# A fifth buffer for the split numerators, a sixth instead of a seventh for x, and another order of the convolution's last stages

## The chip, the cores and the metric

The kernel runs on one core of a Trainium2 chip. The metric is device time in microseconds of one launch; the kernel before was run three times, and one further execution was profiled.

## The reference

Two stages follow each other. The first is a causal convolution over the sequence with 7 taps, whose weights are a softmax per head (8 heads of 24 columns, d_model 192, 8 sequences of 4160 rows). The second treats the 33280 rows as tokens of one SoLU layer with 1024 hidden columns.

```python
w = softmax(weight)                                  # 8 heads x 7 taps
out[b, s, h, :] = sum_k w[h, k] * x_pad[b, s + k, h, :]
x = out.reshape(B * S, D)                            # 33280 x 192
h = x @ w_in                                         # 192 x 1024
sm = exp(h - max(h)); sm = sm / (sum(sm) + 1e-9)
solu = h * sm
ln = (solu - mean(solu)) / sqrt(var(solu) + 1e-6) * g_ln
return ln @ w_out                                    # 1024 x 192
```

## The kernel before, in words

**Tiles and steps.** The tokens are cut into 260 tiles of 128 rows. From tile 8 on, the program is written out by `three_steps(i)` (L1443), which lays down three tiles i, i+1, i+2 (a, b, c below) in an order by hand; one call is a *step* here. For each tile t:

- PE multiplies the convolved rows by w_in into `ph`: `emit_rows` (L860), and a remainder by `emit_quads` (L895) in steps that also convolve, by `emit_third` (L883) in the others. The rows come from `ring`, and the remainder also from `ring2`, a copy of half of one block of `ring` ("the doubled block").
- DVE takes the maximum (L930), ACT the exponential (L937), DVE the product, the numerators `e` (L947).
- ACT casts `e` to f16 into the upper half of `p16` (`emit_hi`, L955); POOL writes what the cast lost into the lower half (`emit_lo`, L967); SP then issues one DMA transpose of all of `p16` into `pT` (L969). So `p16` is free again when that transpose has landed. There are 4 buffers of `p16` and 5 of `pT`.
- PE multiplies `pT` by w_out into `po` (`emit_out`, L999), from tile 26 on for the tiles i-6 to i-4 in step i: the first of them at the step's start, one in its middle, one at its end.

**Chunks.** The convolution works ahead in chunks of 18 tiles (chunk 3 begins at tile 32, chunk 4 at 50, chunk 5 at 68, chunk 7 at 104, chunk 14 at 230; the last, 15, has 12 tiles from 248 on). The six steps of a chunk are a *cycle* here; s is the first tile of the chunk that is being prepared. For a chunk there is, in order of time:

- loads of x, four pieces into buffers `xr` (L190), XR of them, on SP's queue; DVE's sums (L210); a scale;
- POOL splits each piece into two f16 halves: three instructions (L262, L266, L269), laid down from a queue of work whose pace is the number in `queue.run(...)`; the buffer `xr` is free after the third;
- the edge rows: `edge_piece` (L1137) forces what is left of that splitting and issues three small DMAs `room<-xs` (L279) of 6 partitions by 18 slots by 192; there are two pieces r = 0, 1;
- four convolutions of two heads each (`groups`, L293): PE with the bands (L352) and with the edges in `room` (L359), then ACT (L401) and DVE (L410) write `y16`, which has three blocks of 128 columns. Block 0 holds the columns of the heads 0 to 5, block 1 those of the heads 5 to 7 and their remainders, block 2 the remainders of block 0;
- DMA transposes of these blocks into `ring` (`turn`, L437), two parts of 9 tiles for each block, and two copies from `ring` into `ring2` (`double`, L449).

**What sets the order.** All DMAs stand in SP's one queue, in the program's order, and an SP instruction that waits holds all behind it. `plans()` (L1142) decides by a table of tile numbers in which step each of these parts is laid down: the four convolutions at s-18, s-15, s-12, s-9 (`steps`), the edge pieces at s-27. Turns, doubles and edge pieces go through a list from which `three_steps` takes an item after a's `emit_lo`, one after b's and two at its end; edge pieces are taken first. Each DMA also waits for the eighth DMA before it, whose semaphore it uses again.

Of the kernel before, what the change touches and what calls it, by code (L numbers as in the profile page):

```python
# [8 lines left out]
F16 = mybir.dt.float16  # L9
# [11 lines left out]
def kernel(  # L21
# [10 lines left out]
    P = 128  # L32
# [14 lines left out]
    TB = 14  # L47
    TJ = TB + K - 1
    GMAX = 8
    XR = 7  # L50
    DEPTH, LATER = 5, 26


# [73 lines left out]
    class Chunk:  # L127
# [165 lines left out]
        def groups(self):  # L293

            if self.quarter:
                return [(h, 2, 0, 2 * self.m + 1) for h in range(0, H, 2)]
            spans = zip(self.cuts, self.cuts[1:])
            return [hg for a, z in spans for hg in self.heads(a, z)]

# [651 lines left out]

    def emit_hi(t):
        t.halves = t.e.rearrange("p (n f) -> p n f", n=NH)
        t.p16 = sp.tile([P, NH, 2, 512], F16, name=f"p16_{t.i}", tag="p16", bufs=4)
        act.copy(t.p16[:, :, 0, :], t.halves)  # L955

    def emit_square(t):
# [13 lines left out]
    def emit_halves(t, eng):  # L971


        t.halves = t.e.rearrange("p (n f) -> p n f", n=NH)
        t.p16 = sp.tile([P, NH, 2, 512], F16, name=f"p16_{t.i}", tag="p16", bufs=4)
        t.pT = sp.tile([P, 2 * NFC, P], F16, name=f"pT_{t.i}", tag="pT", bufs=5)
        for n in range(NH):
            hi, lo = t.p16[:, n, 0, :], t.p16[:, n, 1, :]
            act.copy(hi, t.halves[:, n])
            eng.tensor_tensor(lo, t.halves[:, n], hi, ALU.subtract)  # L980
            nc.sync.dma_start_transpose(
                t.pT[:, n * NFC : (n + 1) * NFC, :],
                t.p16[:, n].rearrange("p a f -> p (a f)"),
            )
# [157 lines left out]
    def plans():  # L1142
# [17 lines left out]
        for c in chunks[3:]:  # L1160
# [2 lines left out]
            steps = [s + 3 * j for j in (-6, -5, -4, -3)]  # L1163
            if c.ch == 3:
                steps = [20, 23, 23, 26]
            for i, hg in zip(steps, c.groups()):
                at_tile(i, "conv", (c, hg))
            at_tile(steps[2], "open", c)
            p0, p1 = c.parts
            at_tile(steps[2], "turn", *[  # L1170
                lambda c=c, q=q: c.turn(*q)
                for q in ((0, *p0), (0, *p1), (2, *p0), (2, *p1), (1, *p0), (1, *p1))
            ])
            if not c.exact:
                at_tile(steps[0] - (9 if c.ch > 4 else 3), "edge" if c.ch > 4 else "turn", *[
                    lambda c=c, r=r: edge_piece(c, r) for r in range(2)
                ])
            at_tile(steps[2], "turn", *[lambda c=c, q=q: c.double(*q) for q in c.parts])
            if c.ch > 5:
                back = next(t for t in tiles if t.ch == c.ch - 3)  # L1180
                spread_over(back.i, back.i + 0.5 * back.n, "load", [(c, j) for j in range(c.np)])
            if c.ch > 4:
                back = next(t for t in tiles if t.ch == c.ch - 3)
                at, end = (0.25, 0.65) if c.ch > 5 else (0.35, 0.8)
                sums(c, back.i + at * back.n, back.i + end * back.n)

    class Queue:
# [255 lines left out]
    def three_steps(i):  # L1443
# [170 lines left out]
            if not split[1:]:  # L1614
                emit_evac(d)
        run_chain(4)
        queue.run(3.8 if i < 4 * PAIRED else 1.7)
        if start:
            lowers(2)
        emit_square(a)  # L1620
# [36 lines left out]
                emit_square(b)  # L1657
        if PAIRED < i < 2 * PAIRED:
            add(1)
        queue.run(3.8 if i < 4 * PAIRED else 1.7)  # L1660
        if i == 3 * FIRST // P + 2:
            split_bands()
        if i == PAIRED + 3:
# [9 lines left out]
        elif start:  # L1673
            openings()
            doubles.extend(work.get("double", []))
        else:
            opens()
            if not soon:
                turns()
            move(2)  # L1680
            doubles.extend(work.get("double", []))
        if i == NT - 6:
            ready(b)
        if not held:
            queue.run(3.8 if i < 4 * PAIRED else 1.7)
        take_rooted()

    def ready(t):
# [93 lines left out]
```

## Time and profile before

| | |
|---|---|
| median of 3 runs | 1273.02 us (1269.63 to 1274.27) |
| the profiled execution | 1268.97 us, of which the trace's span is 1267.2 us |
| granted TensorE clock, mean | 0.963 |
| PE busy | 1149.0 us, 91% |
| ACT, DVE, POOL busy | 980.1, 956.1, 889.4 us |
| DMA queue of SP | 226.17 MB, 97.2% of 16 engines' span |

The difference between the profiled execution's 1268.97 us and the span lies ahead of the first instruction and behind the last one. Busy shares are of the whole span; a PE that is busy at half its clock counts as busy.

### The profile page before, as it was taken

Reading aid. Unit: us, or ns where it says so; the run is one execution under the profiler, and the core shown is the slowest. Engines: PE = TensorE matmul, PEld = TensorE weight load, DVE = VectorE, ACT = ScalarE, POOL = GpSimd, SP = SyncE. Lnnn points to the kernel's source line nnn. Section 1 sums busy time; section 2 is a strip of 40 time slices with the busy share of each in tenths; the row PEclk is TensorE's granted clock in tenths of the full one; section 3 lists DMA queues with packets and bytes.
Section 4 is the critical chain, followed back from the end, with each engine's and each line's share of the span. In section 5 each row is a group of like instructions: output and inputs, shape, how many; then the busy total and the mean of one; then the engine's idle time right before and its main releaser. Section 6 shows DMA issues by size and latency. Waiting matters only on the chain.

```text
span 1267.2 us, 24734 instructions
## 1 busy us (share of the span) xinstructions
PE 1149.0 (91%) x9070; PEld 684.1 (54%) x9070; DVE 956.1 (75%) x1767; ACT 980.1 (77%) x1739; POOL 889.4 (70%) x755
## 2 busy tenths in 40 slices
PE   5998986988979979989899899997997999999998
PEld 3664543645546545555455465554654655556556
DVE  8878874976858858768588697785885876867776
ACT  7986764866868958778688687785886877868886
POOL 3644592986977769669678687686785977657575
PEclk9998987999999989999999899998999999989999
DMA  8899996899999999999998999999999999898899
GB/s 235 166 179 176 197 170 137 158 149 214 192 153 208 156 211 182 165 206 187 171 198 163 201 198 160 198 189 165 190 150 197 188 156 194 158 191 144 167 192 179
DMA packets 732396, 227.75 MB, mean 180 GB/s; under 512 B 659702, under 2 KB 730226, under 8 KB 732274
## 3 DMA queue, kind: packets, MB, share of 16 engines
q1 hardware_dynamic: 732274, 226.17, 97.2%
q8 instruction: 71, 1.16, 0.4%
q14 instruction: 51, 0.42, 0.1%
HBM read 30.67 MB, written 25.56 MB: 44 GB/s over the span
## 4 chain that ended last, share of the span: by engine, by line
PE 61%; DMA 12%; POOL 11%; issue 5%; ACT 4%; DVE 4%; SPq 3%; POOLq 0%; ACTq 0%; DVEq 0%
PE po L999 27%; PE ph L860 26%; DMA pT<-p 8%; POOL p L967 7%; PE ph L895 3%; ACT p L955 2%; DMA ring<-ring 2%; PE pc L352 2%; SPq L969 2%; DVE ph L930 2%; PE ph L883 1%; PE pc L359 1%; DMA xr<-in_x_dram 1%; POOL xs L269 1%; POOL xr L266 1%
## 5 line engine op out<-in xcount | busy, mean ns | idle before, releaser
L967 POOL TENSOR_TENSOR p<-e,p 128x1024 f16<-128x1024 f32 x257 | 547.3, 2135 | 317.3 <-ACT p L955 314.9
L999 PE MATMUL po<-ohl,pT 128*128 128x192 f16 (+1 forms) x4264 | 553.6, 288 | 39.9 <-DMA pT<-p 39.5
L999 PEld LDWEIGHTS <-pT 128*128 128x128 f16 x4264 | 389.9, 99 | 207.9 <-DMA pT<-p 45.4
L930 DVE TENSOR_SCALAR_CACHE_REDUCE ph<-ph,cv 128x1024 f32<-128x1024 f32 x260 | 335.3, 1291 | 145.3 <-PE ph L895 83.2
L860 PE MATMUL ph<-whi,ring 128*128 128x512 f16 x1548 | 429.0, 387 | 2.6 <-DVE e L947 2.6
L947 DVE SCALAR_TENSOR_TENSOR e<-ph,cv,e 128x1024 f32<-128x1024 f32 x260 | 332.6, 1279 | 76.5 <-ACT e L937 75.9
L937 ACT ACTIVATE e<-ph,sm 128x1024 f32<-128x1024 f32 x260 | 289.8, 1115 | 65.9 <-DVE ph L930 54.4
L860 PEld LDWEIGHTS <-ring 128*128 128x128 f16 x2064 | 195.7, 100 | 229.0 <-issue 38.3
L955 ACT CAST p<-e 128x1024 f16<-128x1024 f32 x257 | 266.7, 1038 | 68.0 <-DMA pT<-p 51.9
L959 ACT ACTIVATE sq<-e 128x1024 bf16<-128x1024 f32 x260 | 274.2, 1055 | 0.2
L860 PE MATMUL ph<-wlo,ring 128*128 128x512 f16 x516 | 157.8, 388 | 0.0
L1009 DVE TENSOR_REDUCE raw<-po 128x192 f32<-128x384 f32 x247 | 137.0, 555 | 18.5 <-PE po L999 18.3
L401 ACT ACTIVATE y<-pc 128x432 f16<-128x432 f32 (+2 forms) x120 | 46.2, 451 | 119.4 <-PE pc L359 119.4
L269 POOL TENSOR_TENSOR xs<-xr,xs 128x960 f16<-128x960 f32 (+2 forms) x47 | 89.8, 1911 | 1.5
L895 PE MATMUL ph<-wlo,ring 64*64 64x512 f16 x612 | 50.9, 405 | 39.5 <-DMA ring<-ring 39.5
L410 DVE SCALAR_TENSOR_TENSOR y<-pc,y 128x432 f16<-128x432 f32 (+2 forms) x120 | 54.2, 502 | 27.7 <-ACT y L401 27.7
L210 DVE TENSOR_REDUCE xa<-xr 128x1 f32<-128x384 f32 (+1 forms) x98 | 58.2, 616 | 12.7 <-DMA xr<-in_x_dram 12.7
L1076 ACT ACTIVATE raw<-raw,t 128x192 f32<-128x192 f32 x127 | 56.4, 447 | 0.0
L1070 POOL TENSOR_TENSOR t<-t,mhalf 128x8 f32<-128x8 f32 (+2 forms) x33 | 53.5, 1622 | 2.6
L895 PEld LDWEIGHTS <-ring 64*64 64x64 f16 x612 | 15.0, 108 | 70.4 <-DMA ring<-ring 43.1
L937 ACT ACTIVATION_READ_ACCUMULATOR e<-ph,sm 128x1 f32 x260 | 51.4, 198 | 0.0
L959 ACT ACTIVATION_READ_ACCUMULATOR sq<-e 128x1 f32 x260 | 50.7, 195 | 0.0
(150 smaller groups left out, 662.2 us busy)
## 6 DMA issues: line engine op xcount, KB each, us to landing
out_dram<-raw SPq DMA_DIRECT2D x63, 384.0 KB
xr<-in_x_dram SPq DMA_DIRECT2D x70, 240.0 KB
xr<-in_x_dram SPq DMA_DIRECT2D x22, 192.0 KB
pT<-p SPq DMA_TRANSPOSE x263
ring<-ring SPq DMA_DIRECT2D x24, 144.0 KB
xr<-in_x_dram SPq DMA_DIRECT2D x6, 480.0 KB
room<-xs SPq DMA_DIRECT2D x66, 40.5 KB
ring<-y SPq DMA_TRANSPOSE x99
```

Of the source, the lines that this page charges most:

```text
L210: dve.tensor_reduce(self.part[:, col : col + 1], self.raw[j][:, a:z, :], AX.XY, ALU.max, apply_absolute_value=True,)
L269: (2.1 * size + 0.2, lambda: pool.tensor_tensor(xl, r, h, ALU.subtract)),
L860: nc.tensor.matmul(bank, lhs, w[:, r, n * 512 : (n + 1) * 512], start=start and j == 0, stop=stop and j == len(ops) - 1,)
L895: nc.tensor.matmul(t.ph[c : c + R, at:end], y[q, t.off + c : t.off + c + R], wlo[q, 1, at:end], start=start, stop=not start,)
L930: dve.tensor_scalar(t.ph, t.ph, t.cv[:, 0:1], None, ALU.mult, ALU.min, accum_out=t.bias)
L937: act.activation(t.e, t.ph, AF.Exp, bias=t.bias, scale=-1.0, accum_out=grp.z[:, g : g + 1])
L947: dve.scalar_tensor_tensor(t.e, t.ph, t.cv[:, 3:4], t.e, ALU.mult, ALU.mult, accum_out=t.grp.s1[:, t.g : t.g + 1],)
L955: act.copy(t.p16[:, :, 0, :], t.halves)
L959: act.activation(junk, t.e, AF.Square, accum_out=t.grp.s2[:, t.g : t.g + 1])
L967: eng.tensor_tensor(t.p16[:, :, 1, :], t.halves, t.p16[:, :, 0, :], ALU.subtract)
L999: nc.tensor.matmul(t.po[:, 0:n], t.pT[:, a, :], w, start=j == 0, stop=j == len(ops) - 1)
L1009: dve.tensor_reduce(t.grp.raw[:, t.g, :], t.po[:, 0 : 2 * D].rearrange("p (a d) -> p d a", a=2), AX.X, ALU.add,)
```

## The change

The numerators' `p16` gets a fifth buffer, and `xr` loses its seventh. A chunk's four convolutions go from the heads 6 and 7 down to 0 and 1, so that block 1 is complete after the second of them; it is turned and doubled then, and blocks 0 and 2 are turned after the fourth. The edge pieces are laid down at s-24 and not at s-27. POOL's splitting gets a smaller pace, DVE's sums a later place, and chunk 4 makes its first two convolutions in one step. The table gives the loads of x a slightly later place too, but from chunk 6 on they come out in the same steps as before.

```diff
@@ -47,7 +47,7 @@
-    XR = 7
+    XR = 6
@@ -293,7 +293,7 @@
             if self.quarter:
-                return [(h, 2, 0, 2 * self.m + 1) for h in range(0, H, 2)]
+                return [(h, 2, 0, 2 * self.m + 1) for h in range(H - 2, -1, -2)]
@@ -951,7 +951,7 @@
-        t.p16 = sp.tile([P, NH, 2, 512], F16, name=f"p16_{t.i}", tag="p16", bufs=4)
+        t.p16 = sp.tile([P, NH, 2, 512], F16, name=f"p16_{t.i}", tag="p16", bufs=5)
@@ -1163,25 +1163,33 @@
             if c.ch == 3:
                 steps = [20, 23, 23, 26]
+            elif c.ch == 4:
+                steps = [s + 3 * j for j in (-5, -5, -4, -3)]
             for i, hg in zip(steps, c.groups()):
                 at_tile(i, "conv", (c, hg))
             at_tile(steps[2], "open", c)
             p0, p1 = c.parts
-            at_tile(steps[2], "turn", *[
-                lambda c=c, q=q: c.turn(*q)
-                for q in ((0, *p0), (0, *p1), (2, *p0), (2, *p1), (1, *p0), (1, *p1))
+            turn = lambda *q, c=c: lambda: c.turn(*q)
+            twice = [lambda c=c, q=q: c.double(*q) for q in c.parts]
+            if c.exact:
+                at_tile(steps[1], "turn", turn(1, *p0), turn(1, *p1), *twice)
+            else:
+                at_tile(steps[1], "turn", turn(1, *p0))
+                at_tile(steps[2], "turn", twice[0], turn(1, *p1))
+                at_tile(steps[3], "turn", twice[1])
+            at_tile(steps[3], "turn", *[
+                turn(*q) for q in ((0, *p0), (2, *p0), (0, *p1), (2, *p1))
             ])
             if not c.exact:
-                at_tile(steps[0] - (9 if c.ch > 4 else 3), "edge" if c.ch > 4 else "turn", *[
+                at_tile(steps[0] - 6, "edge" if c.ch > 4 else "turn", *[
                     lambda c=c, r=r: edge_piece(c, r) for r in range(2)
                 ])
-            at_tile(steps[2], "turn", *[lambda c=c, q=q: c.double(*q) for q in c.parts])
             if c.ch > 5:
                 back = next(t for t in tiles if t.ch == c.ch - 3)
-                spread_over(back.i, back.i + 0.5 * back.n, "load", [(c, j) for j in range(c.np)])
+                spread_over(back.i, back.i + 0.55 * back.n, "load", [(c, j) for j in range(c.np)])
             if c.ch > 4:
                 back = next(t for t in tiles if t.ch == c.ch - 3)
-                at, end = (0.25, 0.65) if c.ch > 5 else (0.35, 0.8)
+                at, end = (0.3, 0.7) if c.ch > 5 else (0.35, 0.8)
@@ -1614,7 +1622,7 @@
-        queue.run(3.8 if i < 4 * PAIRED else 1.7)
+        queue.run(3.8 if i < 4 * PAIRED else 1.45)
@@ -1677,12 +1685,12 @@
-            move(2)
+            move(3 if len(work.get("turn", [])) > 4 else 2)
```

`emit_halves` gets the same fifth buffer as `emit_hi`, and the other two `queue.run` of a step the same 1.45.

**First place: SP's queue in the steps of tiles 95 to 100, ahead of chunk 7 (s = 104).** `pT_96` is tile 96's transpose, `room` the edges of chunk 8, `ring<-y16` a turn and `ring2<-ring` a double, both of chunk 7. Before:

```order
L279 DMA room_77<-xs_8_5141 6x18x192 x3
L969 DMA_TRANSPOSE pT_96_5895<-p16_96_5892 128x16x128
L279 DMA room_77<-xs_8_5141 6x18x192 x3
L969 DMA_TRANSPOSE pT_97_5949<-p16_97_5941 128x16x128
L437 DMA_TRANSPOSE ring_74<-y16_76 128x9x128 x2
L1091 DMA out_0_dram<-raw_80_5220 128x4x192
L969 DMA_TRANSPOSE pT_98_6011<-p16_98_6008 128x16x128
L437 DMA_TRANSPOSE ring_74<-y16_76 128x9x128
L969 DMA_TRANSPOSE pT_99_6038<-p16_99_6035 128x16x128
L437 DMA_TRANSPOSE ring_74<-y16_76 128x9x128
L969 DMA_TRANSPOSE pT_100_6077<-p16_100_6074 128x16x128
L449 DMA ring2_75<-ring_74 64x1152 x2
```

The same queue after the change, from tile 97's transpose on:

```order
L969 DMA_TRANSPOSE pT_97_5937<-p16_97_5929 128x16x128
L449 DMA ring2_75<-ring_74 64x1152
L437 DMA_TRANSPOSE ring_74<-y16_76 128x9x128 x2
L1091 DMA out_0_dram<-raw_80_5213 128x4x192
L969 DMA_TRANSPOSE pT_98_6000<-p16_98_5997 128x16x128
L279 DMA room_77<-xs_8_5135 6x18x192 x3
L969 DMA_TRANSPOSE pT_99_6030<-p16_99_6027 128x16x128
L279 DMA room_77<-xs_8_5135 6x18x192 x3
L969 DMA_TRANSPOSE pT_100_6071<-p16_100_6068 128x16x128
L437 DMA_TRANSPOSE ring_74<-y16_76 128x9x128 x2
```

The edge pieces moved back by three tiles, from behind the transposes of tiles 95 and 96 to behind those of 98 and 99. The last double moved forward from behind tile 100 to behind tile 97, and the first double and both turns of block 1 lie further ahead, behind tiles 91 and 94.

**Second place: SP's queue around the last load of chunk 6 (`xr_6_3`), with what each row waits for.** `DMAHW..` are the semaphores of earlier DMAs; the others are engines. Before:

```order
L969 DMA_TRANSPOSE pT_37_2441<-p16_37_2437 128x16x128 [waits DMAHW2_49,PE_49,Pool_49]
L190 DMA xr_6_3_2449<-in_x_dram 64x4x192 [waits DMAHW3_49]
L190 DMA xr_6_3_2449<-in_x_dram 64x4x192 [waits DMAHW4_49]
L969 DMA_TRANSPOSE pT_38_2563<-p16_38_2560 128x16x128 [waits DMAHW5_49,PE_49,Pool_49]
L969 DMA_TRANSPOSE pT_39_2590<-p16_39_2587 128x16x128 [waits DMAHW6_49,PE_49,Pool_49]
```

After:

```order
L190 DMA xr_6_3_2446<-in_x_dram 64x4x192 [waits DMAHW4_49,Pool_49]
L190 DMA xr_6_3_2446<-in_x_dram 64x4x192 [waits DMAHW5_49]
L969 DMA_TRANSPOSE pT_38_2556<-p16_38_2553 128x16x128 [waits DMAHW6_49,PE_49,Activation_49]
L969 DMA_TRANSPOSE pT_39_2583<-p16_39_2580 128x16x128 [waits DMAHW7_49,PE_49,Activation_49]
L969 DMA_TRANSPOSE pT_40_2633<-p16_40_2625 128x16x128 [waits DMAHW0_49,PE_49,Activation_49]
L449 DMA ring2_75<-ring_74 64x1152 [waits DMAHW3_49,DMAHW1_49]
L437 DMA_TRANSPOSE ring_74<-y16_76 128x9x128 [waits DMAHW2_49,DVE_49]
L1091 DMA out_0_dram<-raw_24_2002 128x4x192
L969 DMA_TRANSPOSE pT_41_2743<-p16_41_2740 128x16x128 [waits DMAHW4_49,PE_49,Activation_49]
L969 DMA_TRANSPOSE pT_42_2770<-p16_42_2767 128x16x128 [waits DMAHW5_49,PE_49,Pool_49]
```

The load now waits for POOL, and the transposes of tiles 38 to 41 behind it no longer name POOL, since that wait covers theirs; tile 42's does again.

**The same place on POOL after the change**, with the split of the piece `xr_5_1`, whose buffer is the one that the sixth load behind it, `xr_6_3`, takes:

```order
L967 TENSOR_TENSOR p16_40_2625<-e_40_2612,p16_40_2625 128x2x512
L967 TENSOR_TENSOR p16_41_2740<-e_41_2731,p16_41_2740 128x2x512
L269 TENSOR_TENSOR xs_5_2163<-xr_5_1_1384,xs_5_2163 128x960
L967 TENSOR_TENSOR p16_42_2767<-e_42_2737,p16_42_2767 128x2x512
L1078 TENSOR_SCALAR raw_24_2002<-raw_24_2002,t2_24_1552 128x192
```

The piece is free only behind tile 41's `emit_lo`; in the order before, with seven buffers, `xr_6_3` takes the buffer of `xr_5_0`, whose split stands behind tile 35's.

## Rows read from the trace of the kernel before

**Rows 1.** PE's waits: for whom, us in total, times, longest.

```profile
PE ph L895 <- DMA ring<-ring: 39.5, 12, 5.3
PE po L999 <- DMA pT<-p: 39.5, 16, 5.3
PE pc L359 <- DMA room<-xs: 10.7, 2, 8.0
```

**Rows 2.** The other engines' waits, in the same columns.

```profile
POOL p L967 <- ACT p L955: 314.9, 110, 20.4
...
ACT p L955 <- DMA pT<-p: 51.9, 26, 4.9
```

**Rows 3.** Steps of one cycle: window: us, busy (instructions), granted clock, DMA share, GB/s.

```profile
479.80:492.60 12.80, 12.80 (x118) 7.72 (x117) 11.31 (x20) 11.26 (x22) 11.12 (x9) 1.00 0.91 188
492.60:505.20 12.60, 12.60 (x118) 7.62 (x116) 11.98 (x23) 11.19 (x21) 12.42 (x11) 1.00 1.04 204
505.20:517.50 12.30, 12.30 (x82) 6.96 (x81) 10.83 (x19) 11.32 (x22) 10.22 (x10) 1.00 1.09 201
517.50:529.60 12.10, 12.10 (x82) 6.98 (x81) 9.23 (x18) 9.98 (x17) 8.78 (x6) 1.00 0.80 74
529.60:550.10 20.50, 14.54 (x116) 8.45 (x115) 10.07 (x21) 10.17 (x18) 13.03 (x13) 0.92 1.09 213
```

**Rows 4.** Whole cycles, cut at the exponential of a chunk's first tile, same columns.

```profile
297.70:382.50 84.80, 76.77 (x625) 45.45 (x624) 63.76 (x116) 65.43 (x116) 65.84 (x54) 0.98 1.04 184
...
466.00:550.10 84.10, 78.14 (x626) 45.71 (x625) 64.08 (x116) 65.59 (x118) 63.30 (x53) 0.97 1.02 183
...
972.60:1055.10 82.50, 76.99 (x630) 45.72 (x629) 62.73 (x114) 65.30 (x117) 65.80 (x54) 0.98 1.01 179
1055.10:1133.70 78.60, 75.56 (x619) 44.72 (x617) 59.04 (x101) 64.57 (x115) 52.12 (x41) 0.97 0.94 176
```

**Rows 5.** PE in order of time: start, us, line, idle before and its end.

```profile
533.68 2.12 PE L999 MATMUL po<-ohl,pT 128*128 128x384 f16 x16
538.89 3.81 PE L999 MATMUL po<-ohl,pT 128*128 128x384 f16 x16 [3.09 <-DMA pT<-p]
...
547.63 0.83 PE L895 MATMUL ph<-wlo,ring 64*64 64x512 f16 x10 [2.87 <-DMA ring<-ring]
...
548.65 0.26 PE L359 MATMUL pc<-room 64*64 64x192 f16 x2
...
554.56 4.08 PE L999 MATMUL po<-ohl,pT 128*128 128x384 f16 x32
```

**Rows 6.** SP's queue in order of time: start, us.

```profile
523.06 2.29 SPq L279 DMA_DIRECT2D room<-xs  x3
525.48 4.64 SPq L969 DMA_TRANSPOSE pT<-p  x1
...
538.36 2.07 SPq L969 DMA_TRANSPOSE pT<-p  x1
...
544.76 1.32 SPq L449 DMA_DIRECT2D ring<-ring  x2
```

**Rows 7.** Stretches of the DMA engines, in the columns of rows 3.

```profile
542.00:546.00 4.00, 2.76 (x14) 1.14 (x12) 0.96 (x3) 1.86 (x5) 4.00 (x5) 0.94 1.14 221
...
557.00:561.00 4.00, 4.00 (x38) 2.18 (x40) 2.63 (x6) 3.23 (x6) 3.65 (x6) 1.00 1.01 268
517.00:530.00 13.00, 13.00 (x86) 7.36 (x85) 9.97 (x22) 10.38 (x17) 9.43 (x7) 1.00 0.77 73
201.00:207.00 6.00, 0.39 (x1) 0.12 (x1) 0.00 (x0) 0.00 (x0) 0.00 (x0) 0.50 0.28 56
```

**Rows 8.** POOL, then PE, around tile 41, in the columns of rows 5.

```profile
253.56 2.14 POOL L967 TENSOR_TENSOR p<-e,p 128x1024 f16<-128x1024 f32 x1 [0.65 <-ACT p L955]
...
257.98 2.01 POOL L269 TENSOR_TENSOR xs<-xr,xs 128x960 f16<-128x960 f32 x1
...
253.38 4.08 PE L999 MATMUL po<-ohl,pT 128*128 128x384 f16 x32
```

More of the change, by code (lines that the diff above doesn't have):

```diff
@@ L974, in emit_halves @@
         t.halves = t.e.rearrange("p (n f) -> p n f", n=NH)
-        t.p16 = sp.tile([P, NH, 2, 512], F16, name=f"p16_{t.i}", tag="p16", bufs=4)
+        t.p16 = sp.tile([P, NH, 2, 512], F16, name=f"p16_{t.i}", tag="p16", bufs=5)
         t.pT = sp.tile([P, 2 * NFC, P], F16, name=f"pT_{t.i}", tag="pT", bufs=5)
@@ L1659, in three_steps @@
             add(1)
-        queue.run(3.8 if i < 4 * PAIRED else 1.7)
+        queue.run(3.8 if i < 4 * PAIRED else 1.45)
         if i == 3 * FIRST // P + 2:
@@ L1684, in three_steps @@
         if not held:
-            queue.run(3.8 if i < 4 * PAIRED else 1.7)
+            queue.run(3.8 if i < 4 * PAIRED else 1.45)
         take_rooted()
```

## The prediction

> **What bounds the kernel now.** I read PE's waits first, then the windows of single steps and of whole cycles, then one disturbed step in order of time on PE and on SP's queue.
>
> PE waits for DMAs alone in any amount: 39.5 us for the doubled block, once in each of 12 cycles, 39.5 us for transposes `pT`, and 10.7 us for the edges in `room`, in one place [rows 1]. ACT waits 51.9 us until a buffer of `p16` is free, and POOL 314.9 us for ACT [rows 2]. The windows say where: four of the steps shown take 12.8, 12.6, 12.3 and 12.1 us at the full clock with PE busy throughout, and the last step of the cycle 20.5 us, of which PE is busy 14.54 at a clock of 0.92 [rows 3]. Whole cycles take (1055.1 - 297.7) / 9 = 84.2 us in the mean of nine [rows 4]. A cycle of six undisturbed steps, the first like the second shown and the last like the 12.1, is 12.8 + 12.8 + 12.6 + 12.3 + 12.1 + 12.1 = 74.7 us. So 9.5 us of each cycle are lost, all in its last step. The cycle from 1055.1 on takes 78.6 us and loses 3.9 [rows 4].
>
> Inside one such step [rows 5]: PE waits 3.09 us for a transpose, its next 16 matmuls of `po` take 3.81 us where 16 took 2.12 just before (the lower of the clock's two levels, 1.2 GHz, for most of them; 1.69 us more), and then it waits 2.87 us for the doubled block. On SP's queue, what came ahead are the two edge pieces, the second issued at 523.06; a tile's transpose behind it holds SP for 4.64 us, until 530.12 [rows 6]. From 517 to 530 the DMA engines moved 73 GB/s, where pure transposes run at 221 [rows 7]. So the edges took 13 x (1 - 73 / 221) = 8.7 us of the queue's capacity while PE still ran at full speed [rows 3, 7], and the wait came a step later, when everything behind them was late. The doubles were the last things behind them, at 544.76 [rows 6].
>
> **How full the queue is.** A cycle of 84.1 us at 183 GB/s is 15.4 MB [rows 4]. By their shapes, 18 transposes of 0.524 MB and six turns of 0.295 make 11.2 MB, 50.7 us at 221 GB/s; the six edge DMAs are 0.25 MB; the remaining 3.95 MB of loads, stores and doubles take 14.7 us at the 268 of a stretch with loads and a store [rows 7]. With 8.7 us for the edges that is 74.1 us in a cycle whose floor on PE is 74.7. The change removes no DMA, so the queue stays nearly full, and a cycle can't fall much below 75 us. What it can change is which of PE's readers stands behind the edges.
>
> While the edge DMAs run alone, the engines' share is 0.28 and they move 56 GB/s [rows 7], as if 4.5 of the 16 worked. The Trainium skill, page "DMA: Bandwidth & Descriptors", section "Rules for kernel authors", says that an outermost dimension under 16 confines a DMA to at most that many engines; an edge DMA's is 6; by that rule, the trace agrees. By that page, as an estimate, the edges would run at 6/16 of 221 GB/s and cost 3.0 us a cycle, so that the queue had 6 us to spare; by the window it is 8.7. I sum by the window, since transposes stood waiting in it.
>
> **The change, part by part.**
>
> *Doubled block sooner.* Block 1's turns and the doubles now lie ahead of the edges, and the last double a step earlier; the 39.5 us [rows 1] go, and no row speaks for a remainder. The turns that end last (blocks 0 and 2, second part) are first read nine tiles into the next chunk, three steps on.
>
> *Edges three tiles later.* They are as long as before, so their end moves by a step, 12.2 us (the mean of 12.3 and 12.1 [rows 3]), plus one double that now lies ahead, 1.32 / 2 = 0.7 [rows 6]: 530.1 + 12.2 + 0.7 = 543.0. Their first reader is L359 in the first step of the next cycle; undisturbed it would have come at 548.65 - 3.09 - 1.69 - 2.87 = 541.0 [rows 5]. So a new wait of 2.0 us, where the old order left over a step. PE is in order, so the step's remaining matmuls queue behind it and DVE, ACT and POOL wait for those. Behind the edges come a transpose, two turns and one more transpose, by their bytes at 221 GB/s 2.4 + 2 x 1.33 + 2.4, so 550.5. The second half of the pair of `po` that reads it starts 554.56 + 2.0 - 548.65 = 7.9 us after L359's due time [rows 5], at 548.9, plus the wait, 550.9: just in time, so the wait for `pT` goes as well. A wait of 2.9 us cost 1.7 us of slower clock in one place and none in the other [rows 5]; I take 1.2, bounds 0 and 1.7. The new cycle is 74.7 + 2.0 + 1.2 = 77.9 us, 6.3 less, and by the bound from the queue not under 74.7 nor, if nothing is gained, over 84.2.
>
> *Fifth `p16`.* A tile's cast now needs the landing of the fifth tile before it, not of the fourth. ACT's 51.9 us [rows 2] were the same lateness seen from ACT, so I add nothing; without it the previous item would not hold, since a cast that waits for a transpose holds up the products PE needs. Bounds: 0 to the 51.9.
>
> *Slower splitting, later sums.* POOL's last split of a chunk now stands right before the edges, up to 2.01 us ahead of the next tile's `emit_lo` [rows 8]; POOL waits 314.9 us for ACT [rows 2], which covers it, and the transpose behind it queues behind the edges anyway. Uncovered it is 2 us a cycle. Heads in reverse cost the same matmuls. Together 0.
>
> *Chunk 4.* Its first convolution moves from the step that follows the edges at once to the next one; the 10.7 us for `room` [rows 1] go, and with them about 2 us of the double ahead of chunk 3. Both convolutions now stand in one step, for which I take back 1.2: 11.5 us, once.
>
> *Six `xr`.* From chunk 7 on the order has each piece split before the load that takes its buffer is reached. Once it has not: `xr_6_3` waits for the split behind tile 41's `emit_lo`, and all of SP's queue behind it, the transposes of tiles 38 to 41. Now tile 41's `emit_lo` ends at 255.7; the split takes 2.01 [rows 8], so the load goes out at 257.7; two loads at 0.66 like the doubles' issue, then the transpose of tile 38, 2.07 to issue [rows 6] and 2.4 to move by the rate above, and it lands at 263.5. PE reads it in the second half of the pair of `po` that starts at 253.38, at 255.4 [rows 8]. So PE waits 8.1 us, with 1.7 for the clock 9.8 us, once. Bounds: 0 (if PE runs that late anyway) and 12, a step.
>
> **The sum.** Nine cycles at 6.3 us: 56.7. The one that ends at chunk 4, with the same edges: 6.3. The one of 78.6 us, with 3.9 to lose: 1.5. Chunk 4: 11.5. `xr_6_3`: -9.8. Together 66.2 us off the profiled execution's 1269.0, which gives 1203; the median of the runs is 4 us above that execution, which gives 1207. I say 1205.
>
> **Rivals.**
>
> A, the forecast: 1205, chance 0.54.
>
> B, the edges hide wholly: the fifth buffer and the step of slack take them up, and neither wait nor clock costs anything. Then 11 cycles gain 3.2 more, 1170. For it: the same windows show PE running through the edges undisturbed. Against it: a queue load of 74.1 us in a cycle of 74.7. Chance 0.13. By the Trainium skill's page above, with its 3.0 us for the edges, this rival would be the likeliest.
>
> C, the queue is the bound: lateness only changes its name, and the transposes behind the edges keep PE waiting. If two thirds of the loss come back, 6.3 of 9.5 us, a cycle takes 81.0 and gains 3.2: ten of them 32, with 1.5, 11.5 and -9.8 together 35 us, 1235. For it: the DMA share is above 1 in most windows [rows 3]. Chance 0.20.
>
> D, slower: L359 waits in each cycle as it did at chunk 4, where the edges were issued one step ahead of it, 10.7 us [rows 1], with 1.7 for the clock. A cycle is then 74.7 + 12.4 = 87.1, 2.9 more than now; ten of them 29, with 9.8 lost and 11.5 gained 27 us more than now, 1298. It decides from the point where the edges land over 7.8 us behind L359's due time (9.5 less 1.7), at 548.8 and not at my 543.0. For it: the edges are as slow as before [rows 7], and their reader comes nearer. Against it: it needs 5.8 us of lateness beyond the shifted queue. Chance 0.06.
>
> E, nothing moves: the gain of the doubles is used up by edges and load, so within 0.5% of 1273, chance 0.07.
>
> **How the numbers follow.** About 0.5% is what a measurement of this kernel can tell from no change. Faster by more: A, B and C, 0.87. Within: E, 0.07. Slower: D, 0.06. The range from 1172 to 1242 holds A, C and about half of B, and leaves out the other half, D and E, 0.2 together. For A alone it is 1190 to 1222, by the clock's bounds, the load's and 1 us of error a cycle.
>
> **What would show it.** Right: no wait of PE for `ring<-ring`; a wait of L359 for `room` about 10 times, some 2 us each; steps ahead of a chunk's first tile near 12 us; cycles of 77 to 79 us; one wait of 7 us or so for `pT` near tile 38, with SP standing on a load. Wrong: PE still waiting over 30 us for `pT` (C), or over 60 for `room` (D); no wait for `room` and cycles under 76 (B). The weakest step is the shift of the edges' end by just one step.

## The result

The changed kernel takes 1255.59 us in the median of three runs (1253.50 to 1256.58), against 1273.02 us: a ratio of 0.9866, 95% interval 0.983 to 0.9902. It is faster, by 17.4 us where 68 were forecast, and the time lies above the range. The profiled execution has a span of 1253.9 us, 13.3 less than before; the other 4 us lie between the profiled execution of before and its median, so the parts below, which are read from profiles, may each come out too small by a share of them.

The waits of the changed kernel, in the columns of [rows 1]; DVE's and SP's queue's stand below PE's:

```profile
PE pc L359 <- DMA room<-xs: 33.2, 11, 5.2
PE po L999 <- DVE y L410: 25.9, 10, 4.3
PE po L999 <- DVE e L947: 11.0, 2, 8.5
...
PE po L999 <- DMA pT<-p: 4.9, 6, 1.6
...
DVE xa L210 <- DMA xr<-in_x_dram: 58.1, 13, 6.2
...
SPq L190 <- POOL xs L269: 24.1, 3, 13.8
```

Of the waits in [rows 1] the 39.5 us for the doubled block in L895 are gone, and of the 39.5 for transposes 4.9 are left. In their place PE waits 33.2 us for the edges in L359, and its `po` waits 25.9 us for DVE's L410, which it did nowhere before. DVE itself stands 58.1 us at its sums of x (L210), where before it stood 12.7:

```profile
DVE xa L210 <- DMA xr<-in_x_dram: 12.7, 8, 5.5
```

The windows of the changed kernel, in the columns of [rows 3] and [rows 4]: nine cycles together, then the first, the second and the last of the six steps of the same cycle as in [rows 3], and the first step behind them:

```profile
295.90:1046.40 750.50, 694.93 (x5634) 406.90 (x5633) 574.64 (x1034) 589.20 (x1038) 570.50 (x478) 0.97 1.04 185
...
459.80:477.80 18.00, 13.80 (x121) 7.80 (x119) 10.61 (x19) 11.97 (x26) 12.74 (x13) 0.99 1.15 210
477.80:493.10 15.30, 14.76 (x113) 8.57 (x114) 11.12 (x21) 11.24 (x20) 10.53 (x7) 0.79 1.07 217
...
530.20:545.90 15.70, 12.50 (x115) 7.56 (x114) 9.93 (x21) 10.09 (x17) 11.68 (x13) 0.99 0.85 115
545.90:561.90 16.00, 15.34 (x121) 8.50 (x119) 10.65 (x19) 11.45 (x23) 10.43 (x11) 0.90 1.04 214
```

The first step of that cycle before, which [rows 3] leave out:

```profile
466.00:479.80 13.80, 13.80 (x120) 7.98 (x119) 10.66 (x19) 11.67 (x23) 7.73 (x9) 0.95 1.11 196
```

The last step of the cycle fell from 20.5 to 15.7 us, as meant; the first rose from 13.8 to 18.0 (16.0 in the next cycle) and the second from 12.8 to 15.3, of which 14.76 us are busy at a granted clock of 0.79. The three between them take 12.7, 12.3 and 12.1 us, as before to 0.1 us. A cycle takes 750.5 / 9 = 83.4 us where it took 84.2. The 13.3 us came from three places: 1.8 up to the first of these cycles (297.7 against 295.9), 6.9 in the nine, and 4.6 behind them (212.1 against 207.5).

**How the lateness got there.** SP's queue of the changed kernel in one such place, in the columns of [rows 6]:

```profile
531.32 2.51 SPq L279 DMA_DIRECT2D room<-xs  x3
533.93 3.46 SPq L969 DMA_TRANSPOSE pT<-p  x1
537.44 2.30 SPq L279 DMA_DIRECT2D room<-xs  x3
539.86 4.71 SPq L969 DMA_TRANSPOSE pT<-p  x1
544.61 2.87 SPq L437 DMA_TRANSPOSE ring<-y  x2
547.60 7.52 SPq L969 DMA_TRANSPOSE pT<-p  x3
555.16 3.04 SPq L190 DMA_DIRECT2D xr<-in_x_dram  x4
```

While the two edge pieces move, the DMA engines carry 55 and 49 GB/s, where pure transposes run at 221 [rows 7]:

```profile
532.80:537.20 4.40, 4.40 (x33) 2.80 (x31) 4.14 (x10) 4.13 (x7) 2.60 (x4) 1.00 0.62 55
538.90:544.30 5.40, 2.57 (x43) 1.37 (x42) 2.06 (x5) 1.67 (x3) 5.40 (x6) 1.00 0.79 49
```

PE in order of time, and DVE, in the columns of [rows 5]:

```profile
541.23 0.24 PE L359 MATMUL pc<-room 64*64 64x192 f16 x1
544.67 0.38 PE L359 MATMUL pc<-room 64*64 64x216 f16 x7 [3.20 <-DMA room<-xs]
...
562.52 2.12 PE L999 MATMUL po<-ohl,pT 128*128 128x384 f16 x16 [1.28 <-DVE y L410]
...
560.03 0.55 DVE L210 TENSOR_REDUCE xa<-xr 128x1 f32<-128x384 f32 x1 [3.28 <-DMA xr<-in_x_dram]
...
561.71 1.25 DVE L410 SCALAR_TENSOR_TENSOR y<-pc,y 128x288 f16<-128x288 f32 x4
```

L359 came due at 541.2 and ran 3.20 us after it could have, at 544.67. Behind the edges in the queue stand a transpose, two turns and three transposes, and only then, at 555.16, the loads of x. DVE was free for its sum of one of them 3.28 us before the sum could run, at 560.03. L410 stands behind that sum in DVE's order and ran at 561.71. `pc`, which L410 reads, and `po` take turns in the same two buffers (L91), so PE's `po` needed what L410 gives back and waited 1.28 us more. So a lateness of the queue reaches PE a second time, by way of DVE; how much of it is the edges', the run without them tells below.

### The profile page after: what moved, and what is told of

The parts are those of the page before. It is cut to its first block, busy times and chain, and to the rows that moved or that the text cites. A ratio compares the mean times of both kernels' runs of the same rounds, so it can differ in the third digit from the quotient of the medians.

```text
span 1253.9 us, 24754 instructions
## 1 busy us (share of the span) xinstructions
PE 1141.1 (91%) x9064; PEld 676.7 (54%) x9064; DVE 956.7 (76%) x1767; ACT 981.3 (78%) x1739; POOL 889.5 (71%) x755
## 4 chain that ended last, share of the span: by engine, by line
PE 49%; POOL 18%; issue 11%; DMA 8%; SPq 5%; DVE 4%; ACT 3%; POOLq 0%; DVEq 0%; ACTq 0%
PE po L999 23%; PE ph L860 21%; POOL p L967 10%; DMA xr<-in_x_dram 3%; POOL xs L269 2%; DMA room<-xs 2%; DMA pT<-p 2%; SPq L969 2%; DVE ph L930 2%; PE ph L895 2%; PE ph L883 2%; ACT p L955 1%; PE pc L352 1%; POOL xs L262 1%; POOL t L1070 1%
## 5 line engine op out<-in xcount | busy, mean ns | idle before, releaser
L999 PE MATMUL po<-ohl,pT 128*128 128x192 f16 (+1 forms) x4264 | 549.8, 286 | 42.8 <-DVE y L410 25.9
L947 DVE SCALAR_TENSOR_TENSOR e<-ph,cv,e 128x1024 f32<-128x1024 f32 x260 | 332.5, 1279 | 39.0 <-ACT e L937 38.4
L210 DVE TENSOR_REDUCE xa<-xr 128x1 f32<-128x384 f32 (+1 forms) x98 | 57.5, 616 | 58.1 <-DMA xr<-in_x_dram 58.1
L410 DVE SCALAR_TENSOR_TENSOR y<-pc,y 128x432 f16<-128x432 f32 (+2 forms) x120 | 54.1, 501 | 42.3 <-ACT y L401 42.3
L359 PE MATMUL pc<-room 64*64 64x216 f16 (+6 forms) x424 | 20.9, 252 | 33.2 <-DMA room<-xs 33.2
L1078 POOL TENSOR_SCALAR raw<-raw,t 128x192 f32<-128x192 f32 x117 | 49.5, 431 | 0.0
```

The source lines that it names most:

```text
L210: dve.tensor_reduce(self.part[:, col : col + 1], self.raw[j][:, a:z, :], AX.XY, ALU.max, apply_absolute_value=True,)
L947: dve.scalar_tensor_tensor(t.e, t.ph, t.cv[:, 3:4], t.e, ALU.mult, ALU.mult, accum_out=t.grp.s1[:, t.g : t.g + 1],)
L999: nc.tensor.matmul(t.po[:, 0:n], t.pT[:, a, :], w, start=j == 0, stop=j == len(ops) - 1)
```

## The experiments

Each takes one part out of the two kernels. "A cycle" is one of the nine, from the window named; times are medians, ratios are against the kernel before.

**Later sums.** To take DVE off the late loads:

```diff
-                at, end = (0.3, 0.7) if c.ch > 5 else (0.35, 0.8)
+                at, end = (0.45, 0.7) if c.ch > 5 else (0.35, 0.8)
```

> The changed kernel with DVE's sums of x (L210) begun at 0.45 of the chunk three back, not 0.3, ended at 0.7 as there. Theory 1 (what is late is the load of x behind the edge pieces in SP's queue; DVE, which runs in order, stands at the sum for it, and PE then waits for DVE's L410): DVE's waits for the loads fall from 58.1 us to under 15, PE's wait of L999 for L410 from 25.9 us to under 8, and with the clock that returns the time falls by 25 to 35 us, to about 1225. Rival (SP's queue is the bound, a wait that is taken away comes back under another name): the two waits fall, others rise by as much, and the time stays within 5 us of 1255.

Measured: 1280.07 us, ratio 1.0033 (1.0016 to 1.0051): slower than both kernels, than the one before by 0.3%, which neither theory had said. Its waits:

```profile
SPq L190 <- POOL xs L269: 57.5, 10, 12.4
...
PE pc L359 <- DMA room<-xs: 49.5, 11, 6.7
PE po L999 <- DMA pT<-p: 37.4, 13, 8.7
...
DVE xa L210 <- DMA xr<-in_x_dram: 18.8, 5, 5.3
```

DVE's wait fell as expected, from 58.1 to 18.8 us, and the wait for L410 left the list. But SP now stands 57.5 us, 10 times, on loads of x whose buffer POOL has not split yet (24.1 us, 3 times, in the changed kernel), and all transposes stand behind it. One of the steps in which that happened takes 23.5 us, where the same step of a cycle takes 12.3 in the changed kernel:

```profile
597.90:621.40 23.50, 20.51 (x115) 11.01 (x116) 13.22 (x22) 13.12 (x23) 11.40 (x10) 0.83 1.11 202
```

So six buffers of `xr` are too few for this, and the test of the first theory had to be made again with seven.

**Edges a step sooner.**

```diff
-                at_tile(steps[0] - 6, "edge" if c.ch > 4 else "turn", *[
+                at_tile(steps[0] - (9 if c.ch > 4 else 6), "edge" if c.ch > 4 else "turn", *[
...
-        queue.run(3.8 if i < 4 * PAIRED else 1.45)
+        queue.run(3.8 if i < 4 * PAIRED else 1.7)
```

> The changed kernel with the edge pieces put back by one step, to nine tiles ahead of the chunk's first convolution, and SP's pace put back from 1.45 to 1.7, from chunk 5 on; the doubled block stays ahead, the fifth buffer of p16 and the sums stay. Theory 1: L359's 33.2 us for the edges go, the loads of x go out as late as before or sooner, so DVE's 58.1 us fall by about half: some 1225 us. Rival (queue is the bound): the waits go back to the transposes pT of the step behind the edges, 30 us or more of them, and the time stays at 1250 to 1265.

Measured: 1244.82 us, ratio 0.9757 (0.9719 to 0.9796), between the two expectations in its time, and in its waits what the rival had said: L359's is down to 0.7 us, but PE waits for transposes again, and a cycle takes 745.3 / 9 = 82.8 us. DVE's stand at its sums fell from 58.1 to 35.5 us, and the wait of `po` for L410 from 25.9 to 11.8:

```profile
PE po L999 <- DMA pT<-p: 52.1, 18, 6.3
PE po L999 <- DVE y L410: 11.8, 8, 3.4
...
292.70:1038.00 745.30, 693.99 (x5632) 407.38 (x5631) 574.48 (x1034) 588.31 (x1038) 573.76 (x480) 0.97 1.04 186
```

**No edges.** In the changed kernel, and later in the kernel before:

```diff
-                nc.sync.dma_start(
-                    edges[to : to + EDGE, 0:k, :], half[src - EDGE : src, 0:k, :]
-                )
+                if self.ch < 5:
+                    nc.sync.dma_start(
+                        edges[to : to + EDGE, 0:k, :], half[src - EDGE : src, 0:k, :]
+                    )
```

> The changed kernel without its edge DMAs from chunk 5 on; this leaves out the edge rows of the convolution's input, whose tile is then read as it stood. Theory 1 (the edges' time in the queue is what makes everything late): cycles of 75 to 77 us, PE's waits for room and DVE's for the loads gone, about 1165 to 1175 us. Rival (the queue is full by its bytes, of which the edges are 2%): DMA waits of over 60 us remain, and the time stays above 1220.

> The kernel before without its edge DMAs from chunk 5 on (the edge rows of the convolution's input are left out, their tile is read as it stood). If the edges made the old order's loss too, which the change then only moved to other readers: PE's waits for the doubled block and for transposes, 79 us together, fall under 20, cycles are 75 to 77 us as in the changed kernel without edges, and the time some 1195 to 1205. If the doubles' late place made a loss of its own: PE still waits over 25 us for them, and the time is over 1225.

Measured: 1181.76 us from the changed kernel, ratio 0.9264 (0.9234 to 0.9295), and 1185.80 us from the kernel before, ratio 0.9303 (0.928 to 0.9327). The nine cycles of the one and of the other:

```profile
292.70:975.20 682.50, 675.33 (x5632) 400.83 (x5631) 573.39 (x1034) 588.11 (x1038) 572.85 (x482) 1.00 1.08 201
...
295.90:977.60 681.70, 676.58 (x5634) 402.04 (x5633) 573.53 (x1034) 587.61 (x1038) 569.87 (x477) 1.00 1.08 200
```

Both take 75.8 us a cycle (75.83 and 75.74), at the full clock and at 200 GB/s where they moved 183 to 185. So the queue was not full by its bytes, as the first theory had it, and the two orders are equal as soon as the edges, 0.25 MB of a cycle's 15.4, are out of them. The edges cost the changed order 7.6 us a cycle and the old one 8.4, which is nearly all that either loses. Even in the old order, with its doubles in their late place, PE's wait for them (L896 is L895, a line was added) falls from 39.5 to 12.5 us:

```profile
PE ph L896 <- DMA ring<-ring: 12.5, 8, 4.2
```

One thing did not go as expected: DVE's waits for the loads, which were to be gone from the changed kernel with the edges, are still 38.6 us (16.2 in the old order without them), and the time is 7 us above its range (that of the old order is 9 us below its own):

```profile
DVE xa L210 <- DMA xr<-in_x_dram: 38.6, 13, 5.7
```

So two thirds of DVE's 58.1 us are there without the edges. But PE's `po` then waits for L410 9.2 us and not 25.9, and a cycle loses nothing by it against the old order. What the edges add is what PE feels.

**Edges from GpSimd's queue.**

```diff
-                nc.sync.dma_start(
+                nc.gpsimd.dma_start(
                     edges[to : to + EDGE, 0:k, :], half[src - EDGE : src, 0:k, :]
                 )
```

> The changed kernel with the edge DMAs issued from GpSimd's queue and not from SP's, at the same places of the program; all else as there. Theory 1 (transposes, turns and loads are late since they stand in one queue behind the edges): transposes move beside the edges, DVE's waits for the loads and PE's for room fall to a third, and the time to 1185 to 1210. Rival 1 (the edges take the DMA engines themselves, from whichever queue): the time stays within 10 us of 1255. Rival 2: GpSimd, busy with splits and lower halves, reaches the issue later, PE waits longer for room, and the time rises to 1270 or more.

Measured: 1250.19 us, ratio 0.9811 (0.9757 to 0.9865): the first rival, within 10 us of the changed kernel. PE's wait for the edges does go, from 33.2 to 1.1 us, but it waits 53.3 us for transposes. The profile's DMA issues give 7.7 us from issue to landing for an edge DMA, and in the 7 us in which a set of them moves the engines carry 96 GB/s while SP's queue, with no edge in it, needs 14.22 us to issue three transposes, 9.16 of them for the first:

```profile
room<-xs POOLq DMA_DIRECT2D x66, 40.5 KB, 7.7
...
534.00:541.00 7.00, 4.67 (x33) 2.77 (x30) 6.10 (x13) 6.23 (x10) 6.74 (x9) 1.00 1.12 96
...
532.51 14.22 SPq L969 DMA_TRANSPOSE pT<-p  x3
```

That first transpose's `p16` was complete at 532.4, so it was not POOL that held it; the second set of edges landed at 541.8 to 542.3. So what the edges take, they take from the transposes on another queue as well. The 96 GB/s hold a store too; from 539 to 541, when it is done, edges and transposes move 12. Two things besides the queue are other than in the changed kernel: POOL spends some 0.6 us on each edge DMA, and the edges' packets are of 4.2 and 2.7 KB, not 384 B.

**Edges as whole rows.** Without padding a row is one packet of 6.9 KB; with it, it was 18 of 384 B:

```diff
-    PITCH = D + 8
+    PITCH = D
```

> The changed kernel with the padding of the edges' tile taken away (a slot of D values instead of D + 8), so that a row of an edge DMA is one piece of 6.9 KB where it was 18 packets of 384 B; bytes, queue, partitions and order as there. Theory A (the 74 us that the edges cost in the run without them go to their many small packets): cycles fall by 4 to 6 us, some 1200 us. Theory B (they go to moving six partitions at a time, however the row is cut): within 8 us of 1255.

Measured: 1242.06 us, ratio 0.9745 (0.971 to 0.978). From its first packet to its last, the two batches of three edge DMAs in the cycle shown take 4.1 and 4.2 us in place of 4.4 and 5.4. In the mean of the nine cycles, by the trace's packets, the edges are under way for 8.4 us of a cycle and not 10.0, 1.5 less; a cycle takes 736.9 / 9 = 81.9 us, 1.5 less too:

```profile
528.50:532.60 4.10, 4.10 (x30) 2.52 (x29) 4.07 (x9) 4.04 (x6) 1.96 (x1) 1.00 0.69 61
534.40:538.60 4.20, 3.27 (x47) 1.62 (x45) 2.77 (x5) 2.38 (x5) 4.10 (x6) 1.00 0.74 57
...
294.00:1030.90 736.90, 694.38 (x5634) 407.22 (x5633) 575.12 (x1034) 589.08 (x1038) 569.52 (x478) 0.98 1.03 188
```

L359's wait fell from 33.2 to 14.2 us; PE's wait for L410 stayed, at 27.5. Between the theories, and nearer to B: the small packets are some 15% of the edges' time, and the cycle gained as much as the edges lost. The rest of their time has two parts of about equal length. In the changed kernel, three edge DMAs first move alone; then the next transpose starts and goes on beside them:

```profile
533.00:535.00 2.00, 2.00 (x14) 1.10 (x13) 1.97 (x6) 2.00 (x4) 0.56 (x1) 1.00 0.24 45
...
541.50:544.00 2.50, 0.00 (x0) 0.10 (x1) 0.51 (x2) 0.00 (x0) 2.50 (x4) 1.00 1.32 36
```

Alone, they keep a share of 0.24 of the engines busy at 45 GB/s. In the second stretch, of the next batch, the share is 1.32 and yet both together move 36 GB/s, where transposes without edges run at 221 [rows 7]: the transpose nearly stands until the last edge has landed. Why is not shown.

**The buffers.** The changed kernel with its buffers as before, and the kernel before with the new ones:

```diff
-    XR = 6
+    XR = 7
...
-        t.p16 = sp.tile([P, NH, 2, 512], F16, name=f"p16_{t.i}", tag="p16", bufs=5)
+        t.p16 = sp.tile([P, NH, 2, 512], F16, name=f"p16_{t.i}", tag="p16", bufs=4)
```

> The changed kernel with its buffers as before (four of p16, seven of xr), the new order kept. If the fifth p16 carries the change, ACT's waits for transposes come back (40 us or more of them), PE's behind them, and the time is 1265 to 1280. If the order alone carries it, PE gains back the 8.5 us that xr_6_3 cost and the time is 1245 to 1252.

> The kernel before with five buffers of p16 and six of xr, its order kept. By the theory that the edges' time in the queue sets the loss, ACT's 51.9 us of waits for transposes fall to under 25 but PE's two waits in the last step of a cycle stay, and SP stands some times on a load whose buffer isn't split yet: 1265 to 1285. If the fifth buffer carries the change: 1255 to 1262.

Measured: 1238.35 us, ratio 0.9715 (0.9679 to 0.9752), and 1274.84 us, ratio 0.9998 (0.9976 to 1.0021). The first lies below both of its expectations, the second is as its first one had it: ACT's wait falls to 11.1 us, PE's two waits stay, at 38.9 and 37.7. The new buffers bring nothing to the old order, and cost the new one 17 us. They cost it all of that before the nine cycles: with the old buffers the first of them begins at 278.4, and not at 295.9, and the nine take 753.7 us, 3.2 more.

```profile
278.40:1032.10 753.70, 698.18 (x5632) 408.09 (x5631) 574.81 (x1034) 589.38 (x1038) 571.92 (x480) 0.97 1.03 184
```

In the changed kernel's queue the place is plain; nothing follows the turn, which was issued by 238.1, until the load at 251.97:

```profile
236.15 1.96 SPq L437 DMA_TRANSPOSE ring<-y  x1
251.97 1.29 SPq L190 DMA_DIRECT2D xr<-in_x_dram  x2
```

The same happens 7.9 us long ahead of a load at 160.04. With seven buffers SP has no such wait. The two buffers were not changed apart; that the cost is `xr`'s is read from SP's stands.

**Later sums, seven `xr`.** The first experiment's line with the old buffers.

> The first experiment (DVE's sums from 0.45 on) with seven buffers of xr and four of p16. There the fourth step of four cycles rose from 12.3 to 16.4 and 23.5 us. If that is SP standing on a load whose buffer the later sums and splits free too late, a seventh buffer takes those steps back under 13.5 us, and the time is some 1245 to 1255, with DVE's waits for loads still under 20 us. If it was the later sums themselves, the steps and the 1280 us stay.

Measured: 1228.10 us, ratio 0.9637 (0.9594 to 0.9679), 10 us better than the same buffers without the later sums; a cycle takes 738.6 / 9 = 82.1 us.

```profile
DVE xa L210 <- DMA xr<-in_x_dram: 6.7, 2, 5.5
...
PE pc L359 <- DMA room<-xs: 48.1, 11, 6.2
```

DVE's wait falls to 6.7 us (47.9 with these buffers), and PE's for L410, 28.5 us there, leaves the list; L359's for the edges rises from 28.7 to 48.1. So the chain from the load over DVE to PE was real, and so was the rival: two thirds of the wait that was taken away came back at the edges' reader, and 15 us of the nine cycles stayed gained.

**Edges sooner, old buffers, and spread.** First the second experiment with the old buffers, then on top of it the six edge DMAs one behind each of six tiles:

```diff
...
+            elif not c.exact:
+                for r in range(2):
+                    at_tile(steps[0] - 9 + 3 * r, "edge", *[
+                        lambda c=c, r=r, q=q: edge_piece(c, r, q) for q in range(3)
+                    ])
...
             if sides_due:
-                return sides_due.pop(0)()
+                sides_due.pop(0)()
```

> The second experiment (edge pieces a step sooner, pace 1.7) with four buffers of p16 and seven of xr. If the buffers cost the same 17 us here as in the changed kernel: 1225 to 1232, no wait of SP for a split ahead of a load. If the fifth p16 carried part of the second experiment's gain: 1238 or more. It is also the control of the next run.

> The kernel of the run ahead of this one, with the six edge DMAs of a chunk issued one at a time behind six successive tiles, from the same tile on, and a turn still allowed behind each, where it was three at a time behind two tiles. Theory 'burst' (two batches of 5 us each put the queue further behind than its slack makes up before the next reader): the lateness is halved, cycles fall by 3 to 5 us, some 1185 to 1200. Theory 'sum' (the queue lacks the edges' 10 us in each cycle, however they are cut): within 8 us of the run ahead.

Measured: 1241.99 us, ratio 0.9741 (0.971 to 0.9772), and 1259.59 us, ratio 0.9882 (0.9855 to 0.9908). The first missed the 17 us: it is 2.8 us better than the second experiment, within the two intervals, with cycles of 746.6 / 9 = 83.0 us, 0.1 more, and a start that gained only 4.4 us (288.3 against 292.7). With six buffers and the quicker pace of 1.7, SP had stood only 12.6 us for splits ahead of loads, not 24.1. So the time is in the range of the other expectation, but what the buffers bring there is 1.3 us of nine cycles. Spreading made it worse. PE's waits, of the first and then of the spread kernel, where two lines were added ahead (L361 is L359):

```profile
PE po L999 <- DMA pT<-p: 49.5, 16, 5.6
```

```profile
PE pc L361 <- DMA room<-xs: 66.9, 12, 7.6
PE po L1001 <- DMA pT<-p: 7.7, 7, 4.4
```

Spread out, the edges no longer make the transposes late, but the last of the six goes out some four tiles later, and L359 waits for it instead: 753.3 / 9 = 83.7 us a cycle. The run moved two things, spacing and end, so it doesn't tell burst and sum apart; it does show once more a lateness that changes its reader.

**Both mends.** The eighth experiment with the unpadded rows.

> The eighth experiment (sums from 0.45 on, seven xr, four p16) with the edges' tile without padding, as in the fifth, where an edge batch of three DMAs took 3.5 us and not 5. If the time follows the edges' time in the queue, the 3 us that a cycle saves there come back nearly whole, and the time is 1200 to 1212, PE's wait for room under 25 us. If other work in the queue takes them up: over 1218.

Measured: 1210.13 us, ratio 0.9489 (0.944 to 0.9537), the best of these and faster than both kernels. A cycle takes 719.7 / 9 = 80.0 us, 2.1 less than in the eighth experiment; by the trace's packets the edges are under way for 8.4 us of it and not 9.8, so their 1.5 us came back whole. (A batch of three takes 4.2 us, not the 3.5 of the expectation.) PE still waits 26.2 us for them, just over what was expected.

```profile
279.40:999.10 719.70, 688.45 (x5632) 403.69 (x5631) 576.07 (x1040) 588.27 (x1038) 571.52 (x483) 0.98 1.07 193
...
PE pc L359 <- DMA room<-xs: 26.2, 11, 4.7
```

**The cycles side by side**, the mean of the nine:

| kernel | a cycle, us | where PE waits most |
|---|---|---|
| before | 84.2 | doubled block, transposes |
| changed | 83.4 | edges, DVE's L410 |
| changed, old buffers | 83.7 | edges, L410 |
| before, new buffers | 84.2 | transposes, doubled block |
| edges sooner | 82.8 | transposes |
| edges sooner, old buffers | 83.0 | transposes |
| edges spread | 83.7 | edges |
| edges from GpSimd's queue | 82.5 | transposes |
| sums later, six `xr` | 86.1 | edges, transposes |
| sums later, seven `xr` | 82.1 | edges |
| whole rows | 81.9 | L410, edges |
| sums later, seven `xr`, whole rows | 80.0 | edges |
| no edges, either order | 75.8 | nothing for long |

But for the one in which SP stands on loads, the kernels down to "sums later, seven `xr`" lie within 2.1 us of each other, and wait in different places. Wherever the edges go out on SP's queue in packets of 384 B, they are under way for 9.8 to 10.2 us of a cycle, by the traces' packets. What moved a cycle further was only less time for the edges: 8.4 us of a cycle with whole rows, none without edges.

## Why the prediction was wrong

**What held.** The floor of a cycle was put at 74.7 us; without edges it is 75.8. The edges' cost was put at 8.7 us by the window; taking them out gives 8.4 back in the old order, and 7.6 in the new. By the Trainium skill's page "DMA: Bandwidth & Descriptors", section "Rules for kernel authors", the prediction had 3.0 us as an estimate; there the measurement decides, and it is for the window. The wait for the doubled block in L895 went wholly (L883 waits for it once, 3.9 us, ahead of the nine cycles), and the transposes' nearly so. L359 came due at 541.2, where 541.0 was forecast, and was to wait some 2.0 us about 10 times; it waited 11 times, 3.0 us in the mean. The fifth `p16` was put at 0, and the old order with both new buffers shows 0 in the nine cycles, 757.4 us with them and without. The prediction's reason for it, that the previous item would not hold without it, was not borne out: four buffers cost the new order 3.2 us in nine cycles.

**The step that failed** is "Edges three tiles later", which made 56.7 of the 66.2 us of the sum: a new cycle of 74.7 + 2.0 + 1.2 = 77.9 us. It measured 83.4, so 6.9 us came from the nine cycles. PE's waits in these nine:

```profile
PE pc L359 <- DMA room<-xs: 27.6, 9, 5.2
PE po L999 <- DVE y L410: 23.9, 9, 4.3
```

That is 3.1 and 2.7 us a cycle, for 2.0 and 0 in the sum; and PE is busy 77.2 us a cycle where it is 75.0 without the edges, at a granted clock of 0.97 and not 1.00, so 2.2 us for the clock's 1.2. These three make 4.7 of the 5.5 us by which the forecast cycle was too short, and more than half of that is a wait that the sum did not have. The working followed what stands behind the edges in SP's queue as far as the transposes and turns, found that "just in time", and stopped there. The next thing in the queue was the loads of x. Their reader is DVE's sum, at a fixed place in its order; behind it stands L410; behind that, PE. The term "Slower splitting, later sums" looked at POOL's cover only and put this at 0. That DVE's stand was worth something on PE is shown by the pair of kernels with the old buffers, which differ in the sums alone: 753.7 to 738.6 us. The loads themselves come out in the same steps as before from chunk 6 on. With edges and pace put back together, the wait for L410 is 11.8 us and not 25.9, and with no edges 9.2; so the edges, where they now lie, make the larger part of it. Which other part of the new order makes DVE stand 38.6 us without them, against 16.2 in the old order, was not tried apart.

The rest is that a lateness of some 8 us doesn't end where its first two readers are served. The prediction had rival C for this, "lateness only changes its name", at 0.20, with 81.0 us a cycle; it named the transposes as the place where it would come back, and there it didn't. C's mechanism was the right one and its size too small. Its argument, that the DMA share is above 1 in most windows, was the wrong one: the share is 1.08 without edges too, and the bytes move faster.

One row was also read wrongly: the prediction took a cycle's first step to be like the second and put all of the 9.5 us into the last one, but in the cycle shown 1.0 of them lies in the first, which takes 13.8 us.

**Six `xr`** were put at -9.8 us, one load that stands on a split. For that load, mechanism and size were right:

```profile
258.31 4.02 PE L999 MATMUL po<-ohl,pT 128*128 128x384 f16 x16 [8.51 <-DVE e L947]
```

PE waits 8.51 us, where 8.1 were forecast, and its 16 matmuls take 1.9 us more than the 2.12 of full speed. (The profile puts the wait down to L947, but the weight load in front of them waits 8.8 us there for a transpose.) What was missed is that SP stands on three loads, 24.1 us in all: with the old buffers the nine cycles begin 17.5 us sooner. Of that, 12.2 us are of the cycle with this load in it (96.0 us against 83.8), and 5.3 lie ahead of it, where SP stands 7.9 us on a load that the prediction does not name. The working took the order's statement for the later chunks and named one exception.

**Chunk 4 and the cycle that ends there** were to give 17.8 us together without the load's loss; with the old buffers the nine cycles begin 19.3 us sooner than before, so the two held together. Apart, chunk 4 gave more than its 11.5, 14.8 us by the first tile of chunk 3, and the cycle behind it less than its 6.3: 4.5 us, 83.8 and not 88.3. So part of the agreement is luck. Behind the nine cycles 4.6 us were gained where 1.5 were forecast.

With the parts at their measured size: 19.3 - 17.5 + 6.9 + 4.6 = 13.3 us, the difference of the two spans.

## What to carry to other kernels

A DMA that keeps a shared queue slow makes lateness for every reader behind it; to move it in the order, follow the queue past the first readers to where it has caught up, loads whose reader stands ahead of other work on its engine included, before a gain is put down. Take the suspect out once, even at the cost of the result: here one such run showed that two orders which wait in quite different places lose the same thing. Then shorten it: one constant, the padding of a row, was worth 13 to 18 us, about as much as the whole change. To see what a transfer costs, follow it to its last packet: the stretch in which it moves alone is only the first half of it here. A buffer taken from one pool to feed another is a change of its own, to be timed by itself.

## What the hardware showed that was not expected

- Three edge DMAs of 6 partitions, 0.12 MB, were under way for 5.0 us in the mean in packets of 384 B, and for 4.2 us in packets of 6.9 KB, with 49 to 61 GB/s for all that moved meanwhile in the batches shown.
- For about half of that time a transpose was under way beside them and nearly stood: 36 GB/s for both, at a DMA share of 1.32.
- Issued from GpSimd's queue they slowed SP's transposes as well: three took 14.22 us to issue, the first of them 9.16.
- A DMA share above 1 is no sign that the queue has nothing to spare: 1.02 went with 183 GB/s in the old order's nine cycles, 1.08 with 200 when the edges were left out.
